# Two cached attentions: query weights in chunks of 1024 columns instead of 512, in one buffer used in turn

## The chip, the cores and the metric

The kernel runs on one core of one Trainium2 chip. The metric is device time in microseconds (us), the median of repeated executions. The core has a matrix engine (PE, with its weight loads listed as PEld), a vector engine (DVE), a scalar engine (ACT), GpSimd (POOL), and a sync engine (SP) that issues the transfers. Sixteen transfer engines move data between HBM and the on-chip memory SBUF; matrix products land in PSUM.

## What is computed

Two attentions over a given cache, each followed by an output projection; the results are concatenated along the last axis.

```python
# A: Hq=32, Hkv=4 (8 query heads share one key/value head); B: H=32, every head its own
# both: B=16, Sq=32, D=1024, Sk=1024, Dh=128, all bfloat16
q = (x @ wq).reshape(B, Sq, 32, Dh).transpose(0, 2, 1, 3)
k, v = ...                        # A: repeated 8 times along the heads; B: as they are
scores = einsum("bhqd,bhkd->bhqk", q, k) * Dh ** -0.5
o = einsum("bhqk,bhkd->bhqd", softmax(scores, axis=-1), v)
out = o.transpose(0, 2, 1, 3).reshape(B, Sq, 32 * Dh) @ wo
concatenate([out_A, out_B], axis=-1)
```

The keys and values of B are 268 MB, those of A 34 MB, and each of the four weight matrices 8.4 MB (1024 x 4096 or 4096 x 1024). All of it is read once.

## The kernel before

**Work units.** Each attention is cut into 128 steps, and the loop at the end of `build` walks through them with a step `t` of B and about 1.03 steps of A at a time. A step handles 128 rows of scores (four batch and head pairs of 32 queries) by 1024 keys. For B, 16 steps make a block `m` of 4 heads (four groups `G` of 128 tokens, 4 steps each). For A, 32 steps make a block `s` of 8 heads, which share one key/value head. In a step, PE makes the scores (L823 for B, L803 for A), DVE takes the row maximum (L833), ACT the exponential (L846), PE transposes the probabilities (L858), ACT or DVE moves them out of PSUM (L525), PE multiplies with the values (L888, L880), and the result is scaled (L904, L905), transposed (L910) and moved (L525). After four steps of B, or eight of A, the output projection runs (L679) and is added to `acc` (L690).

**Query projections.** `qprojA_head` (L597) makes one head of A for all 512 tokens, `qprojB` (L615) four heads of B for 128 tokens. Each is 8 matmuls of 128x512. A's result goes to `QT_sb`, two blocks deep. B's goes to `Qtok`, also two blocks of four slots; `qprepB_tr` (L624) turns it on DVE into `QBt`, and `qprepB_sh` (L637) spreads it with small 32x32 matmuls into one PSUM bank for each `a` in 0 to 3, from where ACT or DVE moves it to `QR` (128x256). One `a` is done in each step. For the next block of B, one `qprojB` is written at steps 0, 3, 6 and 9 of 16; for the next block of A, one head in every four steps.

**Query weights.** `wq_sb` holds one chunk of 512 columns for each attention, 8 KB of every partition for each. `wq_load` fills it with four transfers of 256 KB in rows of 1024 B. The next chunk of an attention goes into the same place, once its last reader is through; the loop defers its load by `LAZY_DELAY`, 4 steps.

**Order.** The program isn't run in the order in which it is written. `list_schedule` plans it: it simulates the engines with durations from `DUR` and transfers with packet times from `PACKET`, and among the operations that could start soonest it takes the one with the largest remaining path, less 3 us for each later step. It also hands out PSUM banks (four for general use, two of which are kept for projections, `BANK_RESERVE`) and chooses ACT or DVE for moves. The order found is then fixed in each engine's queue, with semaphore waits. All transfers are issued by SP, one after the other: a transfer that waits for its buffer holds up all later ones. The planner lets SP issue at most 5 us ahead of the transfers (`SP_AHEAD`).

**Buffers for keys and values.** B's keys have 8 slots of 512 KB (two to a step, `KB_sb`, loaded at L748), B's values 3 slots of 1 MiB (`VB_sb`, L761). A's keys and values have two slots each of 256 KB (L743, L755). `woA_sb` and `woB_sb` hold the output weights of one block (2 MiB in eight transfers at L651, 1 MiB in four at L661).

**Start.** x of both attentions is loaded into the space of `acc` (L533; blocks 1 to 3 wait for the first one), transposed on PE (L545) and moved to `xT_sb`. Then come `qprojB` for block 0, four heads of A, and the loads of A's output weights and of the second chunks of query weights; heads 4 to 7 of A follow at the second step of A.

Of the kernel before, what the change touches and what calls it, by code (L numbers as in the profile page):

```python
# [10 lines left out]
BF = mybir.dt.bfloat16  # L11
# [5 lines left out]
NVB_SLOTS = 3  # L17
NKB_SLOTS = 8
LAZY_PER_STEP = 100
LAZY_DELAY = 4  # L20
A_STEPS_FRAC = 0.97
# [5 lines left out]
PE_MODE = {"scoresB": 2, "Qshuf": 2, "PVB": 1}  # L27
# [3 lines left out]
STEP_NEAR = 0  # L31
ACT_FIRST = 0.3
# [4 lines left out]
    "OT_tr": (0.056, 0.22), "KTA_tr": (0.45, 0.22), "Qshuf": (0.107, 0.20), "qprojA": (0.432, 0.20), "qprojB": (0.432, 0.20),  # L37
    "oprojA": (0.432, 0.20), "oprojB": (0.432, 0.20), "xT_tr": (0.45, 0.22),
    "exp": (1.10, 0.12), "PT_ev@act": (0.466, 0.13), "norm@act": (0.25, 0.13), "OT_ev@act": (0.11, 0.13), "KTA_ev@act": (0.466, 0.13),
    "qA_ev@act": (0.47, 0.13), "qB_ev@act": (0.478, 0.13), "QR_ev@act": (0.252, 0.13), "acc0@act": (0.47, 0.13), "acc0@dve": (0.58, 0.12), "xT_ev@act": (0.90, 0.13),  # L40
# [3 lines left out]
    "qA_ev@dve": (0.58, 0.12), "qB_ev@dve": (0.58, 0.12), "xT_ev@dve": (0.60, 0.12), "o_fin@dve": (0.58, 0.12), "QR_ev@dve": (0.30, 0.12),  # L44
# [3 lines left out]
PACKET = {"kb_dma": (4096, 0.159), "wq_dma": (1024, 0.046)}  # L48
# [57 lines left out]
class Prog:  # L106
# [61 lines left out]
    def _needs_wait(self, op, d):  # L168
        if d.dma_key is not None:
            return True  # L170
        if d.eng != op.eng:
            return True
        return op.eng in self.SELF_SYNC
# [49 lines left out]
    def list_schedule(self, lat=0.05, look=LOOK):  # L223
# [43 lines left out]
        def slot_time(i):  # L267

            t = 0.0
            for v in acq[i]:  # L270
                idle = [slot_free[v.cls][x] for x in range(SLOTS[v.cls]) if held[v.cls][x] is None]
                keep = sum(k for kind, k in BANK_RESERVE.items() if kind != v.kind and not any(h is not None and h.kind == kind for h in held["bank"])) if v.cls == "bank" else 0
                if len(idle) <= keep:
                    return None
                t = max(t, sorted(idle)[0])
            return t
# [34 lines left out]
        while True:  # L311
# [54 lines left out]
            for u in users[best]:  # L366
                uo = ops[u]
                same_pe = (op.dma_key is None and beng == uo.eng and uo.eng == "pe")
                r = free[beng] if same_pe else op.t1 + lat
                if uo.dma_key is not None:  # L370
                    r += DMA_MARGIN.get(uo.name, DMA_MARGIN_DEFAULT)
                if r > ready_t[u]:
                    ready_t[u] = r
                ndeps[u] -= 1
                if ndeps[u] == 0:
                    make_ready(u)
# [54 lines left out]
def build(nc, pa, pb, out):  # L431
# [34 lines left out]
    with stack:  # L466
# [7 lines left out]
        zeros = sb("zeros", [P, P], BF)  # L474
        id32 = sb("id32", [P, P], F32)
        z32 = sb("z32", [P, P], F32)
        stat = sb("stat", [P, SLOTS["stat"], 4], F32)
        xT_sb = sb("xT_sb", [P, 2, DJ, NTOK], BF)
        wq_sb = sb("wq_sb", [P, 2, DJ, CW], BF)
        QT_sb = sb("QT_sb", [P, 2, Bn, HS, Sq], BF)  # L480
        Qtok = sb("Qtok", [P, 2, NG, CW], BF)
# [25 lines left out]
        if HOOK is not None:  # L507
            print("sbuf bytes remaining per partition:", nc.sbuf_bytes_remaining() if callable(nc.sbuf_bytes_remaining) else nc.sbuf_bytes_remaining)

        pr.add("pool", lambda g: g.memset(zeros[:], 0.0), writes=["zeros"], name="c0")  # L510
        pr.add("pool", lambda g: g.affine_select(ident[:], zeros[:], [[1, P]], ALU.not_equal, 1.0, base=0, channel_multiplier=-1),
               reads=["zeros"], writes=["ident"], name="c1")
        pr.add("pool", lambda g: g.memset(z32[:], 0.0), writes=["z32"], name="c0")
        pr.add("pool", lambda g: g.affine_select(id32[:], z32[:], [[1, P]], ALU.not_equal, 1.0, base=0, channel_multiplier=-1),
               reads=["z32"], writes=["id32"], name="c1")
# [38 lines left out]
        def lazy_push(key, thunk):  # L554
            lazy.append((key, thunk, cur_step[0] + LAZY_DELAY))

# [15 lines left out]

        def wq_load(pi, c):
            wq = (pa if pi == 0 else pb)["wq"]
            jp = DJ // WQP
            for k_ in range(WQP):
                def th(k_=k_):
                    pr.add("sp", lambda e: e.dma_start(wq_sb[:, pi, k_ * jp:(k_ + 1) * jp, :],
                                                       wq[k_ * jp * P:(k_ + 1) * jp * P, c * CW:(c + 1) * CW].rearrange("(j p) c -> p j c", p=P)),
                           writes=[("wq", pi, k_)], dma_key=f"wq{pi}_{k_}", name="wq_dma", dur=jp * P * CW * 2,  # L580
                           wtag={("wq", pi, k_): c})
                lazy_push(("wq", pi, c), th)

        def qprojA_head(s_, hh):
            h = s_ * HS + hh
            lazy_flush(("wq", 0, h // MS))
            hc = h % MS
            for t0 in range(0, NTOK, 512):
# [4 lines left out]
                for j0 in range(0, DJ, JS):  # L593
                    def e_qp(e, t0=t0, tn=tn, j0=j0, v=v):
                        last = None
                        for j in range(j0, j0 + JS):
                            last = e.matmul(bank(v)[:, 0:tn], wq_sb[:, 0, j, hc * Dh:(hc + 1) * Dh], xT_sb[:, 0, j, t0:t0 + tn],  # L597
                                            start=(j == 0), stop=(j == DJ - 1))
                        return last
                    pcs = sorted(set(j * WQP // DJ for j in range(j0, j0 + JS)))  # L600
                    pr.add("pe", e_qp, reads=[("wq", 0, k_) for k_ in pcs] + [("xT", 0, t) for t in range(NG)], writes=[v], claims=[("QT", s_ % 2, hh)], name="qprojA",
                           dur=0.225 * JS, rtag=dict((("wq", 0, k_), h // MS) for k_ in pcs))
# [3 lines left out]
        def qprojB(m_, G):  # L606
            lazy_flush(("wq", 1, m_))
# [3 lines left out]
            for j0 in range(0, DJ, JS):  # L611
                def e_qp(e, j0=j0):
                    last = None
                    for j in range(j0, j0 + JS):
                        last = e.matmul(bank(v)[:, 0:CW], xT_sb[:, 1, j, G * P:(G + 1) * P], wq_sb[:, 1, j, :], start=(j == 0), stop=(j == DJ - 1))  # L615
                    return last
                pcs = sorted(set(j * WQP // DJ for j in range(j0, j0 + JS)))
                pr.add("pe", e_qp, reads=[("wq", 1, k_) for k_ in pcs] + [("xT", 1, G)], writes=[v], claims=[("Qtok", m_ % 2, G)], name="qprojB", dur=0.225 * JS,
                       rtag=dict((("wq", 1, k_), m_) for k_ in pcs))
            evac(Qtok[:, m_ % 2, G, :], lambda: bank(v)[:, 0:CW], reads=[], writes=[v, ("Qtok", m_ % 2, G)], name="qB_ev",  # L620
                 wtag={("Qtok", m_ % 2, G): m_}, mul=scale)

        def qprepB_tr(m_, G):
            pr.add("dve", lambda e: e.transpose(QBt[:, :].bitcast(F32), Qtok[:, m_ % 2, G, :].bitcast(F32)),  # L624
                   reads=[("Qtok", m_ % 2, G)], writes=["QBt"], name="QBt_tr", rtag={("Qtok", m_ % 2, G): m_}, wtag={"QBt": (m_, G)})

        def qprepB_sh(m_, G, a_list):
            gp = (m_ * NG + G) % 2
            for a in a_list:
                v = Virt("bank", "pj")  # L630

                def e_sh(e, a=a, v=v):
                    last = None
                    for rg in range(4):
                        e_ = rg // 2
                        rhs = QBt[32 * a:32 * a + 32, :].rearrange("p (hp e x) -> p e hp x", hp=2, e=2)[:, e_, :, :]
                        last = e.matmul(bank(v)[32 * rg:32 * rg + 32, 0:2 * Dh].rearrange("p (hp x) -> p hp x", hp=2),  # L637
                                        ident[32 * a:32 * a + 32, 32 * a:32 * a + 32], rhs, start=True, stop=True,
                                        tile_position=(32 * a, 32 * rg))
                    return last  # L640
                pr.add("pe", e_sh, reads=["QBt", "ident"], writes=[v], claims=[("QR", gp, a)], name="Qshuf", rtag={"QBt": (m_, G)})
                evac(QR[:, gp, a, :, :], lambda v=v: bank(v)[:, 0:2 * Dh].rearrange("p (hp x) -> p hp x", hp=2), reads=[],
                     writes=[v, ("QR", gp, a)], name="QR_ev", wtag={("QR", gp, a): (m_, G)})
# [365 lines left out]
        qprepB_sh(0, 0, [0, 1, 2, 3])  # L1009
# [6 lines left out]
        cur_step[0] = -LAZY_DELAY  # L1016
        wo_loadA(0)
        wq_load(0, 1)
        if NMSB > 1:
            wq_load(1, 1)  # L1020
        pro_heads = list(range(MS, HS))

# [5 lines left out]
        def stepA(qA):  # L1028
            tA = qA.t % (NG * 8)
            if qA.t == min(1, NIT - 1):  # L1030
                for hh in pro_heads:
                    qprojA_head(0, hh)
                if NSB > 1:
                    wq_load(0, HS // MS)
            quadA_all(qA)
            if qA.s + 1 < NSB:
                nst = NG * 8
                for k_ in range(tA * HS // nst, (tA + 1) * HS // nst):
                    qprojA_head(qA.s + 1, k_)
                    h_ = (qA.s + 1) * HS + k_  # L1040
                    if h_ % MS == MS - 1 and (h_ + 1) // MS < HqA // MS:
                        wq_load(0, (h_ + 1) // MS)
# [5 lines left out]
        for t in range(NIT):  # L1048
# [10 lines left out]
            if tn < NIT:  # L1059
# [3 lines left out]
                qprepB_sh(qn.m, qn.G, [t % 4])  # L1063
            if qB.m + 1 < NMSB:
                nst = max(NG * 4 - 4, 1)
                for k_ in range(NG):
                    if tB == (k_ * nst) // NG:
                        qprojB(qB.m + 1, k_)
                        if k_ == NG - 1 and qB.m + 2 < NMSB:
                            wq_load(1, qB.m + 2)  # L1070
# [51 lines left out]
```

## Time and profile before

| | |
|---|---|
| Median of 3 runs | 896.63 us (896.18 to 898.01) |
| Profiled execution | 897.88 us, span of its instructions 896.0 us |
| PE busy | 813.8 us, 91% |
| DVE busy | 740.8 us, 83% |
| ACT busy | 611.8 us, 68% |
| Moved by the transfer engines | 341.66 MB in 153983 packets, 381 GB/s in the mean |
| Query weight transfers | 32 of 256 KB for each attention, some 10 us from issue to landing |
| B's value transfers | 256 of 512 KB, 10.9 us from issue to landing |
| Mean granted clock of PE | 0.992 |

The profile is of one execution. Its times are in us from the first instruction; busy shares are of the span. A row of an engine's groups names the line of the kernel, the engine, the operation and the tiles. "L761 <- PE L888: 88.0, 36, 5.4" says that SP's transfer at line 761 waited for PE's line 888 for 88.0 us in all, in 36 waits, the longest 5.4 us. The transfers' share can go over 1, since packets overlap a little on one engine.

### The profile page before, as it was taken

What the parts mean: (1) busy time and instruction counts of PE and PEld (TensorE: products, weight loads), DVE (VectorE), ACT (ScalarE), POOL (GpSimd) and SP (SyncE); (2) the same over time, 40 slices, a digit from 0 to 9 for tenths busy, and PEclk for the clock granted to TensorE, in tenths of its full rate; (3) what the DMA queues carried; (4) which work ended last, traced back from release to release, by engine and by line L of the source; (5) the groups of instructions that cost most, each with busy time, mean ns of one, the idle gap of its engine ahead of it and who ended that gap; (6) DMA issues with size and microseconds to landing.
All of it is one profiled execution on the core that took longest, in us unless ns stands there. A gap on an engine that the chain in (4) does not pass through costs nothing.

```text
span 896.0 us, 29282 instructions
## 1 busy us (share of the span) xinstructions
PE 813.8 (91%) x12693; PEld 476.3 (53%) x12864; DVE 740.8 (83%) x1047; ACT 611.8 (68%) x1394; POOL 1.1 (0%) x8
## 2 busy tenths in 40 slices
PE   7999999999999999999889999999989988988876
PEld 4355555555555555555545555555546555555543
DVE  0679888879988898878998788888889789898975
ACT  3468877768777576776767576775768767676752
POOL 0000000000000000000000000000000000000000
PEclk9999999999999999999999999999999999999989
DMA  9999999999999999999999999999999999999994
GB/s 324 386 387 394 395 391 385 382 396 389 388 387 390 395 395 378 385 394 395 394 365 388 392 395 396 379 386 394 393 387 372 392 395 394 396 394 395 397 368 145
DMA packets 153983, 341.66 MB, mean 381 GB/s; under 512 B 12544, under 2 KB 28928, under 8 KB 153856
## 3 DMA queue, kind: packets, MB, share of 16 engines
q1 hardware_dynamic: 153856, 339.79, 101.1%
q8 instruction: 101, 1.65, 0.8%
q14 instruction: 26, 0.21, 0.1%
HBM read 337.64 MB, written 2.10 MB: 379 GB/s over the span
## 4 chain that ended last, share of the span: by engine, by line
PE 51%; DMA 18%; DVE 16%; ACT 9%; SPq 3%; issue 3%; DVEq 0%; ACTq 0%
PE ps_s L823 11%; PE ps_g L858 9%; DMA KB_sb<-in_B_k_cache_dram 8%; PE ps_g L679 8%; DVE stat L833 7%; DVE KB_sb L782 5%; ACT P_sb L846 5%; PE ps_g L888 5%; DMA wq_sb<-in_A_wq_dram 4%; PE ps_g L880 4%; PE ps_g L597 4%; PE ps_g L615 3%; DMA VA_sb<-in_A_v_cache_dram 3%; PE ps_s L803 2%; PE ps_g L774 2%
## 5 line engine op out<-in xcount | busy, mean ns | idle before, releaser
L833 DVE TENSOR_REDUCE stat<-ps_s 128x1 f32<-128x1024 f32 x256 | 304.4, 1206 | 48.0 <-PE ps_s L823 33.8
L782 DVE STREAM_TRANSPOSE KB_sb<-KB_sb 128x1024 f32<-128x1024 f32 x256 | 309.8, 1228 | 30.3 <-DMA KB_sb<-in_B_k_cache_dram 28.6
L846 ACT ACTIVATE P_sb<-ps_s,stat 128x1024 bf16<-128x1024 f32 x256 | 286.4, 1121 | 66.8 <-DVE stat L833 63.7
L858 PE MATMUL ps_g<-id,P_sb 128*128 128x128 f32 x1024 | 174.0, 296 | 14.0 <-ACT QR L525 4.5
L858 PEld LDWEIGHTS ps_g<-id,P_sb 128*128 128x128 f32 x1024 | 151.0, 207 | 53.5 <-ACT QR L525 7.4
L823 PE MATMUL ps_s<-KB_sb,QR 32*32 32x512 bf16 x4096 | 161.9, 400 | 15.7 <-ACT P_sb L846 10.7
L525 ACT COPY PT_sb<-ps_g 128x512 f32<-128x512 f32 x232 | 133.6, 594 | 43.8 <-PE ps_g L858 43.0
L904 ACT ACTIVATE O_sb<-ps_g,stat 128x128 bf16<-128x128 f32 x173 | 63.0, 372 | 58.9 <-PE ps_g L888 35.3
L888 PE MATMUL ps_g<-VB_sb,PT_sb 128*32 128x128 bf16 x4096 | 93.1, 221 | 4.6 <-ACT PT_sb L525 1.5
L888 PEld LDWEIGHTS ps_g<-VB_sb,PT_sb 128*32 128x32 bf16 x4096 | 59.3, 96 | 53.4 <-issue 37.9
L823 PEld LDWEIGHTS ps_s<-KB_sb,QR 32*32 32x32 bf16 x4096 | 46.6, 89 | 74.6 <-ACT P_sb L846 17.5
L880 PE MATMUL ps_g<-VA_sb,PT_sb 128*128 128x128 bf16 x1024 | 78.9, 220 | 2.8 <-DMA VA_sb<-in_A_v_cache_dram 1.7
L880 PEld LDWEIGHTS ps_g<-VA_sb,PT_sb 128*128 128x128 bf16 x1024 | 60.6, 98 | 30.3 <-issue 10.3
L615 PE MATMUL ps_g<-wq_sb,xT_sb 128*128 128x512 bf16 x223 | 67.2, 389 | 5.5 <-issue 2.5
L803 PE MATMUL ps_s<-KTA_sb,QT_sb 128*128 128x512 bf16 x182 | 66.5, 384 | 5.5 <-ACT P_sb L846 1.5
L597 PE MATMUL ps_g<-xT_sb,wq_sb 128*128 128x512 bf16 x232 | 65.8, 380 | 5.4 <-issue 1.9
L679 PE MATMUL ps_g<-woB_sb,OTB_sb 128*128 128x512 bf16 x229 | 62.0, 380 | 4.9 <-issue 2.3
L679 PE MATMUL ps_g<-woA_sb,OTA_sb 128*128 128x512 bf16 x243 | 61.0, 380 | 2.7 <-issue 1.3
L910 PE MATMUL ps_g<-ident,O_sb 128*128 128x128 bf16 x256 | 49.9, 222 | 7.6 <-ACT O_sb L904 2.6
L525 ACT CAST QR<-ps_g 128x256 bf16<-128x256 f32 x117 | 43.7, 382 | 18.4 <-PE ps_g L637 14.3
L690 DVE TENSOR_TENSOR acc<-acc,ps_g 128x512 f32<-128x512 f32 x64 | 41.5, 678 | 13.1 <-PE ps_g L679 12.8
L846 ACT ACTIVATION_READ_ACCUMULATOR P_sb<-ps_s,stat 128x1 f32 x256 | 52.1, 204 | 0.0
(40 smaller groups left out, 528.2 us busy)
## 6 DMA issues: line engine op xcount, KB each, us to landing
VB_sb<-in_B_v_cache_dram SPq DMA_DIRECT2D x256, 512.0 KB, 10.9
KB_sb<-in_B_k_cache_dram SPq DMA_DIRECT2D x256, 512.0 KB, 12.1
KA_sb<-in_A_k_cache_dram SPq DMA_DIRECT2D x64, 256.0 KB, 11.1
VA_sb<-in_A_v_cache_dram SPq DMA_DIRECT2D x64, 256.0 KB, 11.4
wq_sb<-in_B_wq_dram SPq DMA_DIRECT2D x32, 256.0 KB, 10.1
wq_sb<-in_A_wq_dram SPq DMA_DIRECT2D x32, 256.0 KB, 9.7
woB_sb<-in_B_wo_dram SPq DMA_DIRECT2D x32, 256.0 KB, 11.1
woA_sb<-in_A_wo_dram SPq DMA_DIRECT2D x32, 256.0 KB, 9.8
```

Source lines behind the costliest of these rows:

```text
L525: return e.copy(dst, src) if hasattr(e, "activation") else e.tensor_copy(dst, src)
L597: last = e.matmul(bank(v)[:, 0:tn], wq_sb[:, 0, j, hc * Dh:(hc + 1) * Dh], xT_sb[:, 0, j, t0:t0 + tn], start=(j == 0), stop=(j == DJ - 1))
L615: last = e.matmul(bank(v)[:, 0:CW], xT_sb[:, 1, j, G * P:(G + 1) * P], wq_sb[:, 1, j, :], start=(j == 0), stop=(j == DJ - 1))
L679: last = e.matmul(bank(v)[:, 0:OUTW], OT[:, gp, hh, :], wo_[:, hh, oh * OUTW:(oh + 1) * OUTW], start=(hh == 0), stop=(hh == nh - 1))
L782: pr.add("dve", lambda e: e.transpose(KB_sb[:, sl, :].bitcast(F32), KB_sb[:, sl, :].bitcast(F32)), writes=[("KB", sl)], name="KBt_tr", rta ...
L803: pr.add("pe", lambda e, u=u: e.matmul(ps_s[:, vS.idx, u, :], qt[:, q.b, q.hh0:q.hh0 + 4, :].rearrange("p a q -> p (a q)"), KTA_sb[:, sl, ...
L823: last = e.matmul(ps_s[32 * cg:32 * cg + 32, vS.idx, g2, :].rearrange("p (s j) -> p s j", s=16), lhsT, rhs, start=(fp == 0), stop=(fp == 3 ...
L833: pr.add("dve", lambda e: e.tensor_reduce(stat[:, vst.idx, 0:1], ps_s[:, vS.idx, :, :], AXIS.XY, ALU.max, negate=True), writes=vS.res + [v ...
L846: return e.activation(dst, src, ACTF.Exp, bias=stat[:, vst.idx, 0:1], scale=1.0, accum_out=stat[:, vst.idx, 1:2])
L858: last = e.transpose(bank(vb)[:, m * P:(m + 1) * P], p32[:, m:Sk // 2:NPK], id32[:])
L880: last = e.matmul(bank(vb)[:, 0:Dh], ptc_of(vPT, c, 0, P), VA_sb[:, kvs, c, :], start=(c == 0), stop=(c == NCH - 1))
L888: last = e.matmul(bank(vb)[32 * a:32 * a + 32, 0:Dh], ptc_of(vPT, c, 32 * a, 32 * a + 32), VB_sb[:, kvs, a // 2, a % 2, c, :], start=(c == ...
```

## The change

- A chunk of query weights has 1024 columns: 2 MiB, in four transfers of 512 KB with rows of 2048 B. `wq_sb` holds one chunk, for both attentions in turn. Its size in SBUF stays 16 KB of each partition. A's very first chunk goes into `woA_sb` instead, so A's first output weights are loaded only after all eight heads of A's block 0 are projected.
- The projections follow a table: `QB0`, `QA0`, `QB1` for the first 32 steps, `QA_T` and `QB_T` for later periods of 32. In a period, A's eight heads are written at steps 3 to 13 and B's eight projections (two blocks) at steps 18 to 28. The load of the next chunk is written after the last projection that reads the old one, deferred by one step (`WQ_DELAY`).
- `Qtok` becomes a ring of 7 slots.
- The shuffles of B's queries are done for a whole group of four steps at once, in two halves (`a` = 0, 2, then 1, 3). Both halves write the same two PSUM banks, the second waits on a semaphore for the first, and two moves of 128x512 take the result to `QR` instead of four of 128x256.
- The planner counts two banks taken at once correctly and has new durations for the shuffles and moves. Query weights are priced like other transfers with rows of 2048 B (0.084 us a packet; before 0.046 us for 1024 B).
- The tiles `zeros` and `z32` are gone: the identity matrices are built in place.

```diff
+NQT = 7
+WQ_DELAY = 1
+QB0 = [0, 3, 6, 9]
+QA0 = [13 + (i * 9) // 8 for i in range(8)]
+QB1 = [24 + (i * 9) // 8 for i in range(8)]
+QA_T = [3 + (i * 12) // 8 for i in range(8)]
+QB_T = [18 + (i * 12) // 8 for i in range(8)]
...
-PACKET = {"kb_dma": (4096, 0.159), "wq_dma": (1024, 0.046)}
+PACKET = {"kb_dma": (4096, 0.159), "wqh_dma": (1024, 0.049)}
...
+        if (d.name, op.name) == ("Qshuf", "Qshuf2"):
+            return True
...
-        wq_sb = sb("wq_sb", [P, 2, DJ, CW], BF)
+        wq_sb = sb("wq_sb", [P, DJ, 2 * CW], BF)
-        Qtok = sb("Qtok", [P, 2, NG, CW], BF)
+        Qtok = sb("Qtok", [P, NQT, CW], BF)
...
+        def wq_res(pi, c, k_):
+            if pi == 0 and c == 0:
+                return [("woA", j) for j in range(k_ * DJ // WQP, (k_ + 1) * DJ // WQP)]
+            return [("wq", k_)]
+
+        def wq_of(pi, c):
+            return woA_sb if pi == 0 and c == 0 else wq_sb
...
-                    pr.add("sp", lambda e: e.dma_start(wq_sb[:, pi, k_ * jp:(k_ + 1) * jp, :],
-                                                       wq[k_ * jp * P:(k_ + 1) * jp * P, c * CW:(c + 1) * CW].rearrange("(j p) c -> p j c", p=P)),
-                           writes=[("wq", pi, k_)], dma_key=f"wq{pi}_{k_}", name="wq_dma", dur=jp * P * CW * 2,
-                           wtag={("wq", pi, k_): c})
-                lazy_push(("wq", pi, c), th)
+                    res = wq_res(pi, c, k_)
+                    pr.add("sp", lambda e: e.dma_start(dst[:, k_ * jp:(k_ + 1) * jp, :],
+                                                       wq[k_ * jp * P:(k_ + 1) * jp * P, c * 2 * CW:(c + 1) * 2 * CW].rearrange("(j p) c -> p j c", p=P)),
+                           writes=res, dma_key=(f"wq{k_}" if dst is wq_sb else f"wqA{k_}"), name="wq_dma", dur=jp * P * CW * 4,
+                           wtag=dict((r_, ("wq", pi, c)) for r_ in res))
+                lazy_push(("wq", pi, c), th, WQ_DELAY)
...
+            for name, aa in (("Qshuf", (0, 2)), ("Qshuf2", (1, 3))):
+                pr.add("pe", lambda e, aa=aa: e_sh(e, aa), reads=["QBt", "ident"], writes=vv, claims=[("QR", gp, a) for a in aa], name=name,
+                       rtag={"QBt": (m_, G)})
+            for b in range(2):
+                evac(QR[:, gp, 2 * b:2 * b + 2, :, :].rearrange("p a hp x -> p (a hp x)"), lambda b=b: bank(vv[b]), reads=[],
+                     writes=[vv[b], ("QR", gp, 2 * b), ("QR", gp, 2 * b + 1)], name="QR_ev",
+                     wtag={("QR", gp, 2 * b): (m_, G), ("QR", gp, 2 * b + 1): (m_, G)})
...
-        cur_step[0] = -LAZY_DELAY
-        wo_loadA(0)
-        wq_load(0, 1)
-        if NMSB > 1:
-            wq_load(1, 1)
...
+        for G in range(NG):
+            plan(QB0[G], qprojB, 1, G)
+        for p_ in range(NIT // PER - 1):
+            at = QB0[-1] if p_ == 0 else (p_ - 1) * PER + (QB1 if p_ == 1 else QB_T)[-1]
+            plan(at, wq_load, 0, p_ + 1)
+            qa = QA0 if p_ == 0 else QA_T
+            qb = QB1 if p_ == 0 else QB_T
+            for hh in range(HS):
+                plan(p_ * PER + qa[hh], qprojA_head, p_ + 1, hh)
+            plan(p_ * PER + qa[-1], wq_load, 1, p_ + 1)
+            for i in range(2 * NG):
+                plan(p_ * PER + qb[i], qprojB, 2 * (p_ + 1) + i // NG, i % NG)
...
                 for hh in pro_heads:
                     qprojA_head(0, hh)
-                if NSB > 1:
-                    wq_load(0, HS // MS)
+                wo_loadA(0)
...
-                qprepB_sh(qn.m, qn.G, [t % 4])
+                    qprepB_sh(qn.m, qn.G)
+            for what in q_plan.get(t, ()):
+                what()
```

## The prediction

> **What bounds the kernel now.** I read the 40 slices of the page first, then its DMA part, then the busy times of chosen windows, then SP's own waits, then the start of the run in order of time. The slices, and the DMA part below them:
>
> ```profile
> DMA  9999999999999999999999999999999999999994
> GB/s 324 386 387 394 395 391 385 382 396 389 388 387 390 395 395 378 385 394 395 394 365 388 392 395 396 379 386 394 393 387 372 392 395 394 396 394 395 397 368 145
> DMA packets 153983, 341.66 MB, mean 381 GB/s; under 512 B 12544, under 2 KB 28928, under 8 KB 153856
> q1 hardware_dynamic: 153856, 339.79, 101.1%
> ```
>
> The transfer engines are full from the first slice to the last but one, and the packets' own times add up to 101.1% of 16 engines' span. So bytes and the price per byte set the time. The packets under 2 KB less those under 512 B are 28928 - 12544 = 16384: 64 query weight transfers of 256 KB in rows of 1024 B. Rates come next (columns: busy time and instructions of PE, PEld, DVE, ACT, POOL, then clock, DMA share, GB/s):
>
> ```profile
> 5.00:10.00 5.00, 3.55 (x17) 1.41 (x16) 0.00 (x0) 2.09 (x3) 0.00 (x0) 1.00 1.03 335
> 80.00:120.00 40.00, 38.40 (x632) 23.32 (x638) 35.94 (x52) 30.45 (x69) 0.00 (x0) 1.00 1.04 395
> 240.00:280.00 40.00, 37.77 (x608) 22.36 (x615) 34.11 (x52) 30.10 (x69) 0.00 (x0) 1.00 1.04 386
> 300.00:340.00 40.00, 36.94 (x611) 22.27 (x619) 36.87 (x51) 30.49 (x71) 0.00 (x0) 1.00 1.04 395
> 860.00:884.00 24.00, 19.59 (x299) 10.45 (x294) 19.04 (x25) 10.31 (x24) 0.00 (x0) 0.86 0.89 318
> ```
>
> In 80:120 and 300:340 no query weights move: 395 GB/s. In 240:280 two chunks do: 386, at the same full share. In 5:10 mostly query weights move: 335. PE is busy 92 to 96% of these windows, so compute has some 5% to spare, not much. SP's waits:
>
> ```profile
> SPq L761 <- PE ps_g L888: 88.0, 36, 5.4
> SPq L761 <- PE ps_s L823: 84.9, 34, 7.1
> SPq L578 <- PE ps_g L597: 5.0, 3, 3.5
> ```
>
> SP spends most of its waiting on V buffers of attention B (line 761), not on query weights (line 578). These waits cost little: from issues and landings in the trace I work out that 4 to 8 us of bytes are queued almost throughout, with lows of 2 to 3 us near 152, 240, 456 and 672 us. In-flight packets fall visibly below 16 for about 1.9 us in all between 20 and 870 us.
>
> **Packets (on the path).** The trace's records give 49.7 ns for a mean packet of 1024 B, 88.5 ns for 2048 B, 164.7 ns for 4096 B. Removed: 16384 x 49.7 = 814.7 us; added: 8192 x 88.5 = 725.4 us. The difference over 16 engines is 89.3 / 16 = 5.6 us. The 64 transfers become 32 of 512 KB; each ends in 16 small packets of 9.2 ns, so 512 x 9.2 / 16 = 0.3 us more goes. A second way: 2.09 MB of 1024-byte rows in 240:280 cost 40 x (395 - 386) / 395 = 0.9 us, times 16.78 / 2.09 = 8 makes 7.3 us, which also holds ordinary stumbles; the 335 GB/s window gives 16.78 MB x (1/335 - 1/395) = 7.6 us, the upper bound. The lower is 0.3 us: all 2048-byte rows of this trace come from contiguous blocks, while the new rows stand 8 KB apart. I take 5.9 us, as the 1024, 2048 and 4096 byte prices lie on one line (about 38 ns per KB plus 11), which speaks for a fixed cost per packet.
>
> The Trainium skill, "DMA: Bandwidth & Descriptors", section "Why small descriptors are slow", gives about 3 cycles of fixed overhead per packet beside one cycle per 32 B; as an estimate from that page, two packets of 35 cycles become one of 67, 4.3% of 50.9 us, so 2.2 us instead of 5.6. The trace's step of 11% disagrees, and I go by the trace.
>
> **The start (on the path).** First chunks double: 4 MiB of query weights stand ahead of K and V instead of 2. The additional 2 MiB is 2.1 MB / 0.39 = 5.4 us of transfer. It isn't new traffic (the old second chunks follow at 20 to 32 us), but it can delay x. Before, x blocks 1 to 3 are issued at 6.4 to 9.6 us behind nine other transfers, PE transposes x at 13.5 to 18.4 and projects at 18.5 to 30.6, and attention B's first scores run at 32.0. If all eight new pieces stand before x, all of this moves 5.4 us, less the 0.9 us by which the first 2 MiB come faster; if the planner lets x in (its rule keeps SP 5 us ahead of the transfers, which admits about five or six such pieces before x is ready), 0 to 1 us. A's pieces that then come late are covered by the 5 us of transposes and the B projections.
>
> Second, A's output weights (8 transfers, 2 MiB, issued at 37.5 to 44.1 us with no reader in front) now wait in SP's order for A's heads 4 to 7, projected on PE up to 47.0 us; behind that wait stand the K and V loads. Bytes issued by 46 us before: x 2, query weights 4, V of B 3, K of B 5, A's K and V 1.5, output weights 3, together 18.5 MiB. Now 16.5, or 17.5 if the K pair freed at 39 us goes early. That is 2.7 to 5.4 us less queue, against a low of 4.5 us in that stretch. So the engines run dry for 0 to 2 us near 48 us, after which the 2 MiB come. For the start I take +1.0 us, ends 0 and +6.
>
> **One buffer in turn (SP, PE).** Each chunk is loaded a step after its last reader and first read three steps (some 20 us) later; a transfer lands in about 10 us. What gets late is a V load queued behind 2 MiB: before, 1 MiB for each attention came about 20 to 30 us apart. The wait for the last reader can block SP, with all K and V loads behind it; the queued 4 to 8 us cover a wait of the longest size seen on this line (3.5 us), and beyond that each us is lost. Six such loads: 0 taken; ends -1.9 (all present stumbles vanish) and +4.
>
> **Projections moved.** The 128 projections by two remain; PE's work is the same (8 matmuls of 0.38 us, 3.1 us each). Before, the dense steps hold 0.25 heads of A and 0.4 of B, 2.0 us a step; now 8 in 12 or 11 steps, 2.1 to 2.3 us. Cover: the step is 6.4 to 7 us and PE idles some 6% of it; without cover, 11 steps x 0.3 us. Taken 0.
>
> **Q in half runs.** 512 shuffles remain. New is that the second half of a group's 16 waits for PE's own first half: everything queued behind on PE (scores, transposes, PV) waits too. No such wait is in the trace; nearest is ACT's QR waiting on the same matmuls, 14.3 us in 25 waits, 0.57 us each. So at most 32 x 0.57 = 18 us of PE, at least 0, since the planner now sets other PE work between. PE's 82 us of idle time cover it; the DMA queue covers a single one. Moves to QR: 117 on ACT of 382 ns and 11 on DVE of 405 become 64 of about 600 (the 128x512 move to Qtok is 603): 49.2 - 38.6 = 10.6 us less, on engines busy 68% and 83%; worth 0. Two banks held together can delay a projection; covered alike. POOL's identity set-up (1.1 us at the start) ends before x has come: 0.
>
> **Sum.** -5.9 + 1.0 + 0 = -4.9 us. The profiled execution took 897.88 us (span 896.0), 1.25 above the median 896.63. So it would take 893.0, and the median 891.7 us.
>
> **Rivals.** (1) *Row size doesn't matter*: the 1024-byte price comes from the 8 KB stride, and the new rows pay it too. Then -0.3 + 1.0: 897.3, no change. For it: the trace has no strided row of 2048 B; against it: the straight line through three sizes. The Trainium skill, same page, "Specifications", names 512 B as enough for line rate; by that rule this rival holds, and the trace (335 against 395 GB/s) disagrees so far. (2) *The start costs what the rows save*: all eight pieces stand before x, first scores come 5.4 us late, the buffers are full by then and the whole delay reaches the transfers' end. -5.9 + 5.4: 896.1, no change. It decides from 4.1 us, where less than 1.8 is left. For it: PE's work, which needs x and the weights, is the chain from 13 to 55 us; against it: the planner sees this path and weighs it. (3) *The shared buffer starves the queue*: six reloads each hold SP 2 us longer than the queue lasts, +12: 902.7 us; decides from 1 us each. Against it: the present single buffers cost 7.0 us of SP waits in all.
>
> **Numbers.** Forecast 0.68 (own range 887.5 to 894.8: packets at 7.6 and stumbles gone, or 3 us more lost at the start); rival 1, 0.06; rival 2, 0.08; rival 3, 0.18. A measurement here tells 0.2%, 1.8 us, from no change. Faster 0.68; same 0.06 + 0.08 = 0.14; slower 0.18. The range takes the forecast and the unchanged cases, 0.82 in all, to 0.2% above the median: 888 to 898.5.
>
> **What will show it.** Right: no packets between 512 B and 2 KB, 395 GB/s also while query weights move, hardware_dynamic's packet time down from 906 us an engine (101.1% of 896.0) to about 900. Wrong: a slice of DMA below 9 in the first three (start), dips near steps 10, 21, 32, 46, 61, 78 and 93 with longer SP waits on line 578's successor (shared buffer), or 2048-byte packets dearer than 90 ns (stride). A tail longer than the present 12 us after the last load would also break it.

## The result and the profile after

The changed kernel took 892.20 us in the median of 4 runs (891.66 to 894.39), against 897.32 us (896.18 to 898.45, 4 runs) for the kernel before. The ratio is 0.9948, 95% interval 0.9925 to 0.997: 0.5% faster, 5.1 us. The forecast was 891.7 us, 4.9 us faster. The profiled execution is the slowest of the four, 894.39 us with a span of 892.3 us, so the two profiles differ by less than the medians do, 3.5 us.

The DMA part of the page, after:

```profile
DMA  9999999999999999999999999999999999999994
GB/s 318 397 395 392 391 393 396 392 389 395 395 366 387 396 395 390 380 393 395 395 393 394 391 393 394 372 395 394 394 378 380 393 395 395 396 394 382 394 374 166
DMA packets 145278, 341.65 MB, mean 383 GB/s; under 512 B 12032, under 2 KB 12032, under 8 KB 145152
...
q1 hardware_dynamic: 145152, 339.79, 100.7%
```

The counts under 512 B and under 2 KB are now equal, so no packet lies between: the 16384 rows of 1024 B are gone. The bytes are the same, and the engines are as full as before (100.7% of 892.3 us is 898.6 us of packets for each engine; before 906). The mean packet of 2048 B takes 88.5 ns by the trace's records, as before, though 8192 of them now come from rows that stand 8 KB apart. The same stretches of time as before, with the busy times and instructions of PE, PEld, DVE, ACT and POOL, the clock, the DMA share and GB/s:

```profile
5.00:10.00 5.00, 1.96 (x9) 0.70 (x7) 0.00 (x0) 1.54 (x2) 0.00 (x0) 1.00 0.95 323
80.00:120.00 40.00, 36.82 (x642) 22.04 (x641) 33.73 (x49) 31.27 (x74) 0.00 (x0) 1.00 1.04 392
...
240.00:280.00 40.00, 37.92 (x609) 22.01 (x607) 34.78 (x51) 29.11 (x66) 0.00 (x0) 1.00 1.01 376
300.00:340.00 40.00, 38.03 (x624) 21.87 (x622) 34.87 (x46) 26.98 (x64) 0.00 (x0) 1.00 1.04 394
...
860.00:884.00 24.00, 19.99 (x357) 11.13 (x357) 18.71 (x27) 11.25 (x27) 0.00 (x0) 0.93 0.78 288
```

In 80:120 a whole chunk of query weights now moves, and the rate is 392 GB/s at full share; the forecast was 395. Before, chunks brought 240:280 down to 386. But 240:280 is now lower, 376, with a share of 1.01: there the engines were short of work for a moment. A second profile of the changed kernel has 1.02 and 379 in the same window, so this is no accident of one execution, and SP's waits between 225 and 275 us are mostly for B's value buffers, and none is for query weights. The largest of them:

```profile
SPq L785 <- PE ps_g L912: 8.0, 2, 5.5
```

In 5:10 the engines are short of work too (0.95, before 1.03). The low share in 860:884 is the end of the loads, which comes earlier: the 339th MB (of 10^6 bytes) lands at 880.4 us, before at 882.7. So the rows do nearly what was forecast, and the new order has weak places of its own. SP's waits over the whole run, and those of PE for its own first half of the shuffles (L658, from the list of what PE sat idle for at that line):

```profile
SPq L785 <- PE ps_g L912: 68.3, 33, 6.2
SPq L785 <- PE ps_s L847: 60.3, 30, 7.8
...
SPq L594 <- PE ps_g L912: 0.9, 1, 0.9
```

```profile
  PE ps_g L658: 5.4, 19
```

SP waits for the shared query weight buffer (L594) once, for 0.9 us; before, the two separate buffers cost 7.0 us. PE waits for itself 19 times, 0.28 us each.

The start looks very different. PE in order of time, before and after (start, duration, line):

```profile
30.57 0.73 PE L637 MATMUL ps_g<-QBt,ident 32*32 32x256 bf16 x12
...
32.04 1.12 PE L823 MATMUL ps_s<-KB_sb,QR 32*32 32x512 bf16 x32 [0.15 <-ACT QR L525]
```

```profile
20.11 3.61 PE L615 MATMUL ps_g<-xT_sb,woA_sb 128*128 128x512 bf16 x16
...
32.80 5.89 PE L615 MATMUL ps_g<-xT_sb,woA_sb 128*128 128x512 bf16 x26
...
40.22 0.70 PE L658 MATMUL ps_g<-QBt,ident 32*32 32x256 bf16 x16
...
41.81 1.13 PE L847 MATMUL ps_s<-KB_sb,QR 32*32 32x512 bf16 x32
```

B's first scores come at 41.8 us in place of 32.0, since the planner now sets all eight heads of A in front of them: the 64 matmuls of L615. Yet the same bytes had arrived as early as before: the 16th MB at 44.9 us (before 45.2), the 30th at 80.8 (before 81.4). Order was changed, not work: the fourth step of B begins at 54.3 us, before at 57.4.

### The profile page after: what moved, and what is told of

Same layout as the page of the kernel before. It is cut to its first block, busy times and chain, and to the rows that moved or that the text cites. A ratio compares the mean times of both kernels' runs of the same rounds, so it can differ in the third digit from the quotient of the medians.

```text
span 892.3 us, 29320 instructions
## 1 busy us (share of the span) xinstructions
PE 820.2 (92%) x12864; PEld 469.4 (53%) x12864; DVE 739.5 (83%) x1030; ACT 608.6 (68%) x1347; POOL 1.1 (0%) x8
## 2 busy tenths in 40 slices
DMA packets 145278, 341.65 MB, mean 383 GB/s; under 512 B 12032, under 2 KB 12032, under 8 KB 145152
## 3 DMA queue, kind: packets, MB, share of 16 engines
q1 hardware_dynamic: 145152, 339.79, 100.7%
## 4 chain that ended last, share of the span: by engine, by line
PE 53%; DMA 18%; DVE 14%; ACT 9%; SPq 3%; issue 1%; DVEq 0%; ACTq 0%
DMA KB_sb<-in_B_k_cache_dram 14%; PE ps_s L847 12%; PE ps_g L703 9%; PE ps_g L882 9%; ACT P_sb L870 6%; DVE stat L857 6%; DVE KB_sb L806 6%; PE ps_g L912 5%; PE ps_g L615 4%; PE ps_g L904 4%; PE ps_s L827 3%; PE ps_g L634 3%; PE ps_g L798 2%; ACT PT_sb L531 2%; SPq L785 2%; DMA VB_sb<-in_B_v_cache_dram 1%
## 5 line engine op out<-in xcount | busy, mean ns | idle before, releaser
L847 PE MATMUL ps_s<-KB_sb,QR 32*32 32x512 bf16 x4096 | 160.1, 397 | 23.1 <-ACT P_sb L870 17.4
L882 PEld LDWEIGHTS ps_g<-id,P_sb 128*128 128x128 f32 x1024 | 149.1, 207 | 48.1 <-issue 9.2
L531 ACT COPY PT_sb<-ps_g 128x512 f32<-128x512 f32 x238 | 138.2, 593 | 50.9 <-PE ps_g L882 49.8
L928 ACT ACTIVATE O_sb<-ps_g,stat 128x128 bf16<-128x128 f32 x186 | 67.9, 371 | 62.9 <-PE ps_g L912 36.5
L827 PE MATMUL ps_s<-KTA_sb,QT_sb 128*128 128x512 bf16 x256 | 87.0, 383 | 4.2 <-ACT P_sb L870 4.1
L634 PE MATMUL ps_g<-wq_sb,xT_sb 128*128 128x512 bf16 x256 | 72.8, 388 | 3.9 <-DMA wq_sb<-in_B_wq_dram 3.9
L703 PE MATMUL ps_g<-woB_sb,OTB_sb 128*128 128x512 bf16 x256 | 67.6, 380 | 3.4 <-ACT PT_sb L531 1.3
L934 PE MATMUL ps_g<-ident,O_sb 128*128 128x128 bf16 x256 | 52.5, 223 | 4.5 <-ACT O_sb L928 3.6
L615 PE MATMUL ps_g<-xT_sb,wq_sb 128*128 128x512 bf16 x192 | 55.5, 380 | 0.4 <-ACT QR L531 0.2
L531 ACT COPY OTA_sb<-ps_g 128x64 f32<-128x64 f32 x114 | 24.5, 216 | 37.2 <-PE ps_g L934 36.6
## 6 DMA issues: line engine op xcount, KB each, us to landing
KA_sb<-in_A_k_cache_dram SPq DMA_DIRECT2D x64, 256.0 KB, 12.3
```

The source lines that it names most:

```text
L531: return e.copy(dst, src) if hasattr(e, "activation") else e.tensor_copy(dst, src)
L615: last = e.matmul(bank(v)[:, 0:tn], w_[:, j, hh * Dh:(hh + 1) * Dh], xT_sb[:, 0, j, t0:t0 + tn], start=(j == 0), stop=(j == DJ - 1))
L703: last = e.matmul(bank(v)[:, 0:OUTW], OT[:, gp, hh, :], wo_[:, hh, oh * OUTW:(oh + 1) * OUTW], start=(hh == 0), stop=(hh == nh - 1))
L827: pr.add("pe", lambda e, u=u: e.matmul(ps_s[:, vS.idx, u, :], qt[:, q.b, q.hh0:q.hh0 + 4, :].rearrange("p a q -> p (a q)"), KTA_sb[:, sl, ...
L847: last = e.matmul(ps_s[32 * cg:32 * cg + 32, vS.idx, g2, :].rearrange("p (s j) -> p s j", s=16), lhsT, rhs, start=(fp == 0), stop=(fp == 3 ...
L882: last = e.transpose(bank(vb)[:, m * P:(m + 1) * P], p32[:, m:Sk // 2:NPK], id32[:])
```

## Experiments

Two theories stood against each other on the size of the gain. By the packets' own times, rows are worth 5.6 us. By the bytes that arrive, they are worth less, since short packets overlap more. This is seen in the kernel before, in 2 us of nothing but query weights and 2 us of nothing but rows of 2048 B:

```profile
8.00:10.00 2.00, 1.33 (x10) 0.90 (x10) 0.00 (x0) 0.59 (x1) 0.00 (x0) 1.00 1.09 368
13.00:15.00 2.00, 1.55 (x15) 1.56 (x16) 0.43 (x1) 0.48 (x1) 0.00 (x0) 1.00 1.05 386
```

The share is packet time over 16 engines' time, and over 1 it is overlap: 1.09 with 1024 B, 1.05 with 2048 B. The third theory was that the stride, not the row, sets the price. The runs below were made on three chips; each chip ran the kernel before as well, and the ratios are to that.

**Rows alone, in the kernel before.** Each transfer takes one block of 128 rows by 1024 columns in place of two by 512; bytes, buffers, counts and order are kept. The projections then get weights from the wrong places, so only the time means something; the same holds for the two other runs that change rows alone.

```diff
-  wq_sb[:, pi, k_ * jp:(k_ + 1) * jp, :],
-  wq[k_ * jp * P:(k_ + 1) * jp * P, c * CW:(c + 1) * CW].rearrange("(j p) c -> p j c", p=P)
+  wq_sb[:, pi, k_ * jp:(k_ + 1) * jp, :].rearrange("p j c -> p (j c)"),
+  wq[j_ * P:(j_ + 1) * P, (c // 2) * 2 * CW:(c // 2 + 1) * 2 * CW]      # j_ = k_ * jp + c % 2
```

> The kernel before, every operation and its order kept, only the query weight transfers read rows of 2048 bytes (one block of 128 rows by 1024 columns in place of two blocks by 512; the same 256 KB into the same place, so the projections use mixed up weights and the output is not the reference's). Theory of the row price (5.6 us from the packets' own times): 5 to 6 us faster than before, ratio about 0.9938. Theory of overlap (packets of 1024 bytes overlap more: between 8 and 10 us of the profile before, 183 of them end in each 0.5 us, 375 GB/s, against 95 of 2048 bytes, 389 GB/s, between 13 and 15.5 us): rows are worth 16.78 MB x (1/375 - 1/389) = 1.6 us, ratio about 0.998, and the rest of the change's 5 us comes from its schedule. Theory of the stride: 0.

Measured: 893.65 us (892.63 to 894.92) against 897.84 of the kernel before, ratio 0.9952 (0.9939 to 0.9964). So 4.2 us, between 3.2 and 5.5: the stride theory falls, and so does the overlap theory in its size; the row price of 5.6 stands just outside.

**The change without its rows.** The mirror image: the changed kernel's order, with rows of 1024 B.

```diff
-  dst[:, k_ * jp:(k_ + 1) * jp, :],
-  wq[k_ * jp * P:(k_ + 1) * jp * P, c * 2 * CW:(c + 1) * 2 * CW].rearrange("(j p) c -> p j c", p=P)
+  dst[:, k_ * jp:(k_ + 1) * jp, :].rearrange("p j (u c) -> p (j u) c", u=2),
+  wq[j_ * P:(j_ + 2 * jp) * P, c_:c_ + CW].rearrange("(j p) c -> p j c", p=P)
+                                        # j_, c_ = 2 * jp * (k_ % 2), (2 * c + k_ // 2) * CW
```

> The changed kernel, every operation and its order kept, only the query weight transfers read rows of 1024 bytes (four blocks of 128 rows by 512 columns in place of two by 1024; the same 512 KB into the same place, so the output is not the reference's). Theory of the row price: all of the gain goes, 897.5 to 898 us, ratio to before about 1.000. Theory of overlap: 1.6 us go, 893.8 us, ratio about 0.996. Theory of the stride: unchanged at 892.

Measured: 896.95 us (894.99 to 898.74), ratio 0.9989 (0.9978 to 0.9999). Against the changed kernel on the same chip (below), rows are worth 4.5 us here. What is left for everything else in the change, the 32 transfers fewer included, is 0.9 us, just clear of nothing. The two parts add up: 0.9952 x 0.9989 = 0.9941.

```profile
DMA packets 153470, 341.65 MB, mean 381 GB/s; under 512 B 12032, under 2 KB 28416, under 8 KB 153344
...
q1 hardware_dynamic: 153344, 339.79, 100.8%
```

28416 - 12032 = 16384 short rows again, and the mean rate is that of the kernel before. Since the order is kept, a window can be compared too. 102:118 holds most of one chunk for A; with rows of 1024 B, and in the changed kernel:

```profile
102.00:118.00 16.00, 13.16 (x276) 8.39 (x277) 12.31 (x20) 13.72 (x32) 0.00 (x0) 1.00 1.06 374
```

```profile
102.00:118.00 16.00, 14.07 (x284) 9.03 (x282) 13.13 (x21) 14.05 (x34) 0.00 (x0) 1.00 1.04 391
```

The engines are full in both. With the longer rows the share is lower, and the rate is higher.

**The change again**, as the measure on this chip.

> The changed kernel once more, as the measure for the others on this chip: 891.5 to 893 us, ratio to before 0.994 to 0.996.

Measured: 892.43 us (891.53 to 894.41), ratio 0.9942 (0.9929 to 0.9954).

The account of these profiles, worked out from the trace's packets for 16 engines (overlap is packet time beyond 16 packets in flight, short is what is missing to 16):

| Profile | Packet time | Overlap | Short | Span |
|---|---|---|---|---|
| before | 905.4 | -32.5 | +23.0 | 896.0 |
| before, rows of 2048 B | 897.6 | -30.4 | +25.2 | 892.3 |
| changed, rows of 1024 B | 903.9 | -31.9 | +24.6 | 896.5 |
| changed (second profile) | 897.6 | -30.3 | +22.5 | 889.8 |

Rows cut packet time by 6.3 to 7.8 us, more than the 5.6 worked out, since the mean times of all packets shift a little between profiles (2048 B: 88.5 ns before, 88.3 in the second and fourth row). Overlap gives 1.6 to 2.0 of that back. The shortfall rises by 2.2 us in one pair and falls by 2.1 in the other, and it varies by 1.6 us between two profiles of the changed kernel alone (24.1 and 22.5), so its differences are not read here. The account shows the size of the overlap, then, but doesn't split the measured 4.2 and 4.5 us exactly. Of the 23.0 us short before, 15.7 lie in the first 20 us and after 870 us; the other 7.3 hold the 1.9 that the prediction counted as visible, and many short gaps.

**The old shuffles in the changed kernel.** One `a` in each step, one bank, one move of 128x256, and the planner's old durations.

```diff
-                    qprepB_sh(qn.m, qn.G)
+                qprepB_sh(qn.m, qn.G, [t % 4])
```

> The changed kernel with the old shuffles of B's queries: one a in each step, one bank and one move of 128x256 for each, the planner's old durations for them. Theory of the row price: the shuffles are off the path, within 1.5 us of the changed kernel (the planner's order shifts a little). Rival, the half runs relieve ACT and DVE of 10.6 us and that is a part of the gain: 2 us or more slower than the changed kernel. Rival, PE's wait for itself costs: 2 us or more faster.

Measured: 891.69 us (890.21 to 893.58), ratio 0.9925 (0.9912 to 0.9938), 0.7 us below the changed kernel by the medians, 1.5 us by the ratios, with overlapping intervals. The planner's order changes along with the shuffles here, so this run isn't a change of one thing alone. The half runs don't help; whether they cost up to some 1.5 us is left open.

**Rows of 4096 B in the changed kernel.** One block of 128 rows by 2048 columns for each transfer, order kept.

```diff
+  dst[:, k_ * jp:(k_ + 1) * jp, :].rearrange("p j c -> p (j c)"),
+  wq[j_ * P:(j_ + 1) * P, c_:c_ + 4 * CW]      # j_, c_ = k_ * jp + c % 2, (c // 2) * 4 * CW
```

> The changed kernel, every operation and its order kept, only the query weight transfers read rows of 4096 bytes (one block of 128 rows by 2048 columns; the same 512 KB into the same place, so the projections use mixed up weights). A fixed cost per packet: 4096 packets of 164.5 ns replace 8192 of 88.3, (723.4 - 673.8) / 16 = 3.1 us by the packets' own times; with the share that came through between 1024 and 2048 bytes (4.3 of 5.6 us) 2.4 us: 890 us, ratio to before about 0.9915. Rival, the gain ends at 2048 bytes: as the changed kernel, 892.4 us, ratio 0.994.

Measured: 890.45 us (889.43 to 891.49), ratio 0.992 (0.9908 to 0.9932). At the changed kernel's ratio of 0.9942 it would be 892.4 on this chip, so some 2.0 us are gained; the scaled estimate was 2.4, and the two intervals overlap by a hair. The window 102:118 goes on in the same direction:

```profile
102.00:118.00 16.00, 13.77 (x266) 8.26 (x255) 12.55 (x20) 13.35 (x31) 0.00 (x0) 1.00 1.03 399
```

The gain goes on beyond 2048 B, at about half the size. A kernel that computes the right thing from such rows would need 32 KB of each partition for a chunk in place of 16; that wasn't tried.

**PE held up at the start.** The late first scores had cost nothing. Was the start free, then?

```diff
+  n_ = 19 if (s_, hh, j) == (0, 3, 0) else 1      # 47 in the longer run
+  for i_ in range(n_):
       last = e.matmul(..., start=(j == 0), stop=(j == DJ - 1 or i_ + 1 < n_))
```

> The changed kernel with PE held up once at the start: the first matmul of A's head 3 is done 18 times more (18 x 0.22 = 3.9 us), so all of attention starts that much later; transfers, order and result are the same. If a late start only eats into the queue of transfers (3.1 to 3.8 us at its lowest between 40 and 64 us): 0 to 1 us slower than the changed kernel. If the start is on the path to the end: 3.9 us slower, ratio to before about 0.9985.

> The same with 46 matmuls more, 10.1 us. If a late start only eats into the queue: what goes beyond its 3 to 4 us is lost, 6 to 7 us slower than the changed kernel, ratio to before about 1.001. If compute also catches up afterwards: less, 2 to 5 us. If the start is on the path: 10 us, ratio 1.005.

Measured: 895.63 us (893.77 to 898.20), ratio 0.9978 (0.9968 to 0.9988), and 901.83 us (900.23 to 902.60), ratio 1.004 (1.0027 to 1.0053). Against 892.4 that is 3.2 us of 3.9, and 9.4 of 10.1. So some 0.7 us of each hold don't arrive at the end, with about 1 us of uncertainty, and the 6.2 us that the longer hold has more arrive in full: beyond about 1 us the start is on the path to the end. Windows of the longer run:

```profile
40.00:45.00 5.00, 5.00 (x25) 2.29 (x24) 1.07 (x1) 0.00 (x0) 0.00 (x0) 1.00 0.81 309
45.00:50.00 5.00, 5.00 (x37) 2.21 (x35) 0.00 (x0) 2.25 (x5) 0.00 (x0) 1.00 0.00 1
50.00:55.00 5.00, 4.91 (x91) 1.87 (x91) 3.86 (x4) 3.84 (x7) 0.00 (x0) 1.00 0.97 288
...
80.00:100.00 20.00, 19.21 (x320) 11.23 (x320) 17.24 (x28) 14.92 (x34) 0.00 (x0) 1.00 1.04 392
```

Before 45 us all that was issued has arrived; from 45 to 50 us next to nothing moves. SP's waits say why. In the longer run, from 30 to 56 us (the line is L767 in the changed kernel):

```profile
SPq L769 <- PE ps_g L800: 15.1, 1, 15.1
```

and in the changed kernel itself, from 30 to 50 us:

```profile
SPq L767 <- PE ps_g L798: 3.8, 1, 3.8
```

SP stands at one load of A's keys. Its slot is free once PE has transposed the keys that stand in it, which PE does after A's eight heads. All later loads stand behind this one, the last piece of B's output weights among them, whose space isn't in use yet. In the changed kernel the same three windows have shares of 1.03, 1.04 and 1.03: the 3.8 us are just covered. It passes this place with almost nothing to spare, which the queue worked out in the prediction's manner (lows of 3.1 to 3.8 us between 40 and 64 us) doesn't show.

**PE held up in the middle.** The same hold at head 3 of A's block 2, near 300 us (the edit is shown against the run before).

```diff
-  n_ = 19 if (s_, hh, j) == (0, 3, 0) else 1
+  n_ = 19 if (s_, hh, j) == (2, 3, 0) else 1      # 47 in the longer run
```

> The changed kernel with PE held up once in the middle: the first matmul of head 3 of A's block 2 (near 300 us) is done 18 times more, 3.9 us, as in the run that held the start. If the margin is the depth of the transfer queue at that place (7.6 to 8.8 us near 296 us in a profile of the changed kernel): 0 to 0.5 us slower than the changed kernel, against 3.2 us at the start. If compute bounds the kernel everywhere: 3 to 4 us slower, ratio to before about 0.998.

> The same with 46 matmuls more, 10.1 us. Margin of the queue: the 2 to 4 us beyond it are lost, 894 to 896 us, ratio to before about 0.997. Compute bounds everywhere: 9 to 10 us slower, ratio about 1.004.

Measured: 894.64 us (893.72 to 896.53), ratio 0.9964 (0.9952 to 0.9976), and 898.97 us (897.70 to 900.84), ratio 1.0009 (1.0 to 1.0018). The changed kernel would take 892.9 here by its ratio, so 3.9 us cost about 1.8 (the intervals overlap by a hair), and 10.1 cost about 6. Neither theory's number came: more of a delay is absorbed than at the start, but less than the queue at that place. The longer run shows where it is lost:

```profile
300.00:315.00 15.00, 15.00 (x112) 7.30 (x113) 4.42 (x7) 4.05 (x11) 0.00 (x0) 1.00 1.04 395
315.00:350.00 35.00, 33.51 (x545) 19.61 (x546) 31.06 (x42) 24.61 (x58) 0.00 (x0) 1.00 0.93 334
```

```profile
SPq L787 <- PE ps_g L914: 12.3, 2, 6.2
```

PE is held from about 299 to 309 us, and the transfers don't notice it until 315. Then they fall to 334 GB/s, while SP waits 12.3 us (of the stretch 295 to 330) for two of B's value buffers. The changed kernel itself, in the same 35 us:

```profile
315.00:350.00 35.00, 34.06 (x517) 18.96 (x525) 30.69 (x44) 26.27 (x60) 0.00 (x0) 1.00 1.04 395
```

35 x (395 - 334) / 395 = 5.4 us, most of the 6. It is hardly made up: against the second profile of the changed kernel the 150th MB lands 7.0 us later, the 300th 6.0. For the shorter run the place isn't shown. It is full for 50 us after the hold, and low at 350:360:

```profile
300.00:350.00 50.00, 48.46 (x700) 27.08 (x699) 40.94 (x56) 34.68 (x79) 0.00 (x0) 1.00 1.04 395
350.00:360.00 10.00, 9.63 (x172) 5.26 (x170) 8.45 (x11) 5.46 (x14) 0.00 (x0) 1.00 0.94 336
```

But two profiles of the changed kernel, without any hold, differ there nearly as much between themselves, the second one first:

```profile
350.00:360.00 10.00, 9.27 (x163) 5.56 (x162) 9.18 (x13) 6.98 (x16) 0.00 (x0) 1.00 1.04 385
```

```profile
350.00:360.00 10.00, 9.59 (x185) 5.32 (x169) 8.88 (x11) 5.83 (x14) 0.00 (x0) 1.00 1.01 365
```

So 350:360 is a thin place of this order, and that the 3.9 us were lost there is a guess.

**The shared buffer loaded later.**

```diff
-WQ_DELAY = 1
+WQ_DELAY = 3
```

> The changed kernel with WQ_DELAY 3 in place of 1: each of the six later chunks of query weights is written into the order two steps (some 14 us) later, one step before its first reader. The wait for the shared buffer's last reader gets shorter still, and the chunk lands later (11 us after its issue). If the shared buffer's early reload was what cost: up to 2 us faster than the changed kernel. If the three steps of lead are needed: PE waits some 5 us for each chunk, of which the queue covers 4 to 6; 0 to 6 us slower.

Measured: 892.63 us (892.07 to 893.11), ratio 0.9943 (0.9931 to 0.9955): as the changed kernel. PE's matmuls for B wait 3.4 us for query weights in all, its weight loads 5.8; in the changed kernel 3.9 and 5.3. In both kernels the matmuls' part lies wholly in the first 20 us, where the first chunk comes. One step of lead is enough, and the reload isn't what costs.

## Why the prediction came out right

- **The sum** was 4.9 us, the measurement 5.1. But its terms were off in opposite directions: the rows' 5.6 forecast, 4.2 and 4.5 measured; everything besides them -0.3 + 1.0 = +0.7 forecast, -0.9 measured. So the total was nearer than its parts, and that it came within 0.2 us is luck. The lower end of the forecast's own range isn't what its terms give: 891.7 less 1.7 (packets at 7.6) and less 1.9 (stumbles) is 888.1, not 887.5.
- **Packets** (5.6 + 0.3 us). The mechanism holds in both directions, each with the order kept. The size was set too high by about a quarter. What failed in this term is that packets' times were summed as if they filled the engines alike; the account above shows 1.6 to 2.0 us less overlap, which would leave 3.6 to 4.0 of the 5.6. That is of the right size, but that overlap is the whole of the difference isn't shown, since single profiles move by about 2 us in their other terms. The 0.3 us for 32 transfers fewer was not measured by itself. The second way, by rates (7.3 and 7.6 us), was further off, since its windows also held stumbles that have nothing to do with rows.
- **The fixed cost per packet** was a straight line through three sizes. Rows of 4096 B gave 2.0 us of the 3.1 it promises: right in kind, again smaller.
- **Rival 1, the stride,** is shown wrong by the first run, whose rows stand 8 KB apart like those of the change. The Trainium skill, "DMA: Bandwidth & Descriptors", section "Specifications", has 512 B as enough for line rate; here 1024 B ran at 368 GB/s and 2048 B at 386. Its section "Why small descriptors are slow" led to an estimate of 2.2 us in the prediction; 4.2 to 4.5 were measured, so the overhead here is about twice that.
- **The start, and rival 2.** Taken +1.0, of two steps. In the first, x or A's late weights would hold up the first scores by up to 6 us; they came 9.8 us later, for another reason (the order of A's heads), and it cost no transfer time. In the second, 1 to 2 MiB less would be issued by 46 us and the engines would run dry for 0 to 2 us; 17.25 MiB were issued, in place of 18.5, and 45:50 has a share of 1.04 at 396 GB/s, so its low end came. Rival 2's price didn't come, though the first scores came later than it asked. Holding PE then showed that its mechanism is real: beyond about 1 us, each us at the start is one at the end. The changed order stays just inside.
- **One buffer in turn.** Taken 0. SP's waits at its line fell from 7.0 to 0.9 us, and a later load changed nothing. Rival 3 is wrong as it was put. Weak places in the new order exist (240:280 above), without SP waiting on this buffer.
- **Q in half runs.** Taken 0 within 0 to 18 us of PE; 5.4 us were seen, and undoing it brought no loss, and a gain that noise can explain. The moves to QR took 37.0 us (51 of 600 ns on ACT, 13 of 667 ns on DVE, busy 28.5 and 8.5), the forecast 38.6.
- **Projections moved.** Taken 0, but the working was wrong in size. It counted 8 x 0.38 = 3.1 us of PE for one projection. The profile's rows overlap, and 16 matmuls run in 3.61 us, so one projection takes 1.8 us. It was also covered by "PE idles 6%". The holds show that such idle time is a poor cover: at the start next to nothing of a delay is made up, in the middle some 2 to 4 us.

## What to carry to other kernels

Where transfers bound a kernel, doubling a row from 1024 to 2048 B is worth its measured time even for 5% of the bytes; test it alone by letting the same transfers read the same number of bytes in other rows, with the order untouched. Sum packet times only with a deduction for overlap. A full queue is no proof of slack: hold the suspected engine up for a known time, and see what of it arrives at the end. Take more than one profile of the same kernel before a dip of a few us is put down to a change.

## What the runs showed of the hardware

Packets of 1024 B overlap more on the engines than those of 2048 B (share 1.09 against 1.05), so their own durations, 49.7 and 88.5 ns, exaggerate the difference. With the engines full and the order kept, a window with one chunk of query weights in it moved 374, 391 and 399 GB/s with rows of 1024, 2048 and 4096 B. And transfers that are full hide a stopped PE for a while: held from 299 to 309 us, it brought them down from 315 us on, by 5.4 us in the next 35.
